# Gated linear attention with an MLP on one core: another order table for all five engines

## The chip, the cores and the metric

One Trainium2 chip, one core. The metric is the device time of one execution in microseconds (us); the time of the kernel before is the median of 3 runs.

## The reference

Inputs `q, k, v, a_re, a_im` have the shape (4, 8, 768, 48): batch, heads, sequence, head width, all fp32. Then there are `moe_g_ln` (384), `moe_w_ch1` (384, 1536) and `moe_w_ch2` (1536, 384). Cut to what is computed:

```python
mag   = sqrt(a_re**2 + a_im**2)
scale = minimum(mag, 0.999) / (mag + 1e-6)
a     = (a_re + 1j*a_im) * scale            # a complex gate for each step and channel
for t in range(768):                        # S: state, 48 x 48 for each batch and head
    S = a[t][:, None] * S + outer(k[t], v[t])
    y[t] = q[t] @ real(S)
x   = concat_heads(y)                       # (4, 768, 384)
xn  = (x - mean(x)) / sqrt(var(x) + 1e-6) * g_ln
out = x + maximum(xn @ w_ch1, 0) @ w_ch2
```

## The kernel before, in words

The sequence is cut into chunks of 128 steps, so the 4 batches of 768 steps give 24 chunks, numbered 0 to 23. Two chunks of a batch make a pair: 12 pairs, 0 to 11. Within a chunk the recurrence becomes matrix products; from chunk to chunk a state `G` is carried. The elementwise work on gates, queries and keys is done for a pair at a time (128 x 768). Pair 0 is cut in two halves by heads, so that the first work can start early.

The operations of a pair P (chunks n = 2P and 2P+1), with the names that the table uses:

- Loads: `are`, `aim` (gates, in two copies so that real and imaginary lanes stand side by side), `k`, `q`, `vf`. The weights come with `wl`.
- Magnitude of the gate, as a logarithm: `ln`, `iv` (ACT), `r`, `r2` (the ratio and its square), `u` (ACT), `l`, `lc` (DVE; `lc` is the instruction at L475, `r` and `r2` at L295 or L464).
- `dec` (PE, L483) sums the logarithms along the chunk with a triangular matrix `u_e`; `e` and `en` (ACT, L487) are the exponentials.
- Phase: `th` (arctangent, ACT), `ph` (PE sums it), `car` (the carry for the next pair), `sin`, `abs` (the tile `sh`) and `cos` (ACT; written to `trig`).
- `ke`, `qe` are keys and queries times the decay, `ks`, `qs` these times sine and cosine. DVE or POOL does them (L295). `v` casts the values.
- For each chunk: `qT`, `kT` are transposes on PE (L614) into PSUM, which `qsT`, `ksT` copy out; or `qsT` or `ksT` alone is one transposing DMA on SP's queue (L619). `am` (L637) multiplies queries and keys, `atm` masks the product, `gm` and `G` carry the state, `y` (L687, L690) forms the result, `x` copies it out, `bn` takes mean and variance, `xtr` (L708) and `xT` transpose it, on PE and by a copy, or by a DMA.
- For the pair: `rstd` (L724, L725 on ACT), the first layer `mm1` (L742) in three thirds of two parts, `relu` of each third (L759 on ACT, L761 on DVE; tile `h`), the second layer `mm2` (L774) for each chunk in three parts.
- Output of a chunk: either `ot` on DVE (L790), which scales, adds x and reads PSUM, or `oa` on ACT (L780) and then `ot` on POOL (L787). `st` (L797) stores it.

Nothing in the program chooses the order. A long string, `PLAN`, holds one token for each operation, `name:EngineBank@behind`, in the order in which all engines are to take them. The engine letter is P, A, V, G or S (PE, ACT, DVE, POOL, SP); the digit is the PSUM bank; `@x` makes a POOL operation wait until the DVE operation x is done. DMAs are issued by the engine in the token: on SP's or ACT's or POOL's queue, in that engine's order. `Graph.run` walks the string, emits each operation and asserts that what it needs stands ahead of it. A scheduling layer beneath adds the semaphores, and so every engine runs its own list in order and waits where it must. This layer is the same for both kernels, and it also puts in the waits between two engines that read one PSUM bank. The number of buffers of each tile is set by `RINGS`, which is the same in both.

PE has dummy matmuls besides, `warm.i` (L807), which fill the time before its first real work:

```python
for i in range(134):
    g.add(f"warm.{i}", lambda i=i: nc.tensor.matmul(
        bank(f"warm.{i}")[:, 0:256], lhsT=u_e[:, 0, 0], rhs=..., start=True, stop=True), ...)
```

An operation whose token is missing from the table is left out where the program has two ways to do a thing (`qT`, `kT`, `xtr`, `oa`, `tab`, `warm`): with `qsT.14:S` there is no `qT.14`, with `ot.13:V` no `oa.13`.

Of the kernel before, what the change touches and what calls it, by code (L numbers as in the profile page):

```python
# [54 lines left out]
warm.98:P2 decc.1:V4 warm.99:P2 vf.0.0:S car0.0:G warm.100:P2 warm.101:P2 warm.102:P2 mask:G warm.103:P2 warm.104:P2
aim.3.0:S tab.trig.1:A warm.105:P2 warm.106:P2 warm.107:P2 wl.0:G qe.1.0.1:V warm.108:P2 warm.109:P2 vf.0.1:S
warm.110:P2 warm.111:P2 warm.112:P2 qe.1.0.0:V warm.113:P2 warm.114:P2 pad.qs.1:G warm.115:P2 warm.116:P2 l.2.0:V
th.0.0:A warm.117:P2 warm.118:P2 wl.2:G warm.119:P2 ph.0.0:P1 th.0.1:A th.1.0:A qe.0.0.0:V ph.0.1:P4 qe.0.1.0:V
warm.120:P0 warm.121:P0 warm.122:P0 k.1.0:S car.0.0:V1 decc.0:V5 sin.0.0:A1 lc.2.0:V sin.0.1:A4 qt.0.0:P1 ks.0.0.1:V
warm.123:P0 car.0.1:A4 wgc:V cos.0.0:A1 qt.0.1:P4 ph.1.0:P6 k.1.1:S ks.0.1.1:V cos.0.1:A4 qs.0.1.1:V th.2.0:A  # L60
qs.0.0.1:V qs.0.1.0:V wp.1:P5 ks.0.1.0:V sin.1.0:A6 qs.0.0.0:V ks.0.0.0:V qT.1:P4 wc.1.2:V5 tab.log.2:A qT.0:P1
qsT.1:V4 kT.1:P0 qs.1.0.1:G@wc.1.2 dec.2.0:P2 car.1.0:V6 ln.3.0:A warm.124:P4 qsT.0:V1 warm.125:P4 wp.0:P4 e.2.0:A2
are.4.0:S wc.1.0:V5 kT.0:P1 en.2.0:A2 vf.1.0:S ksT.1:V0 ksT.0:A1 wc.0.0:V4 vf.1.1:S am.1:P2 warm.126:P0 wc.1.1:V5
iv.3.0:A warm.127:P0 am.0:P0 wc.0.2:V4 qt.1.0:P6 tab.trig.3:A warm.128:P5 warm.129:P5 warm.130:P5 warm.131:P5
wc.0.1:V4 warm.132:P5 warm.133:P5 atm.0:V0 ph.2.0:P4 r.3.0:G@wc.0.1 cos.1.0:A6 k.2.0:S v.0:A wp.2:P6 atm.1:V2
aim.4.0:S sin.2.0:A4 gm.0:P7 ke.1.0.0:G y.0:P0 G.0:V7 k.2.1:S x.0:A0 qt.2.0:P4 ke.1.0.1:V gm.1:P7 cos.2.0:A4 y.1:P1
q.2.0:S qs.1.0.0:V xtr.0:P0 ks.1.0.0:V x.1:A1 qT.2:P3 th.3.0:A ks.1.0.1:V qT.3:P5 qsT.2:V3 xtr.1:P1 q.2.1:S xT.0:A0
r2.3.0:G@ks.1.0.1 kT.3:P4 qsT.3:A5 xT.1:V1 kT.2:P2 ksT.3:V4 mm1.0.0.0:P0 G.1:V7 q.3.1:S tab.log.4:A v.1:G am.3:P4
ksT.2:V2 mm1.0.0.1:P0 are.5.0:S ke.2.0.0:G atm.3:V4 ln.4.0:A mm1.0.1.0:P2 q.3.0:S wl.3:G mm1.0.1.1:P2 relu.0.0:A0
wc.2.0:V6 am.2:P4 wc.2.2:V6 relu.0.1:A2 gm.2:P7 k.3.0:S atm.2:V4 ph.3.0:P0 qe.2.0.0:G@wc.2.2 G.2:A7 k.3.1:S iv.4.0:A  # L70
y.3:P2 wl.4:G wc.2.1:V6 y.2:P3 x.3:A2 gm.3:P7 pad.ks.2:G u.3.0:A mm1.0.2.0:P4 x.2:V3 r.4.0:G@wc.2.1 bn.3:V xtr.2:P6
xtr.3:P3 mm1.0.2.1:P4 xT.2:A6 xT.3:V3 G.3:V7 tab.trig.5:A mm1.1.1.0:P2 relu.0.2:V4 qe.2.0.1:G are.6.0:S mm1.1.1.1:P2
sin.3.0:A0 wl.5:G mm1.1.2.1:P6 bn.0:V vf.2.0:S relu.1.1:A2 mm1.1.0.1:P4 pad.qs.2:G l.3.0:V mm1.1.2.0:P6 abs.3.0:A0
r2.4.0:V mm1.1.0.0:P4 th.4.0:A car.3.0:V0 mm2.0.0:P2 relu.1.0:A4 ke.2.0.1:V mm2.1.0:P3 qs.2.0.1:V vf.2.1:S cos.3.0:A
lc.3.0:V mm2.2.0:P4 qs.2.0.0:V bn.2:V tab.log.6:A qT.4:P5 mm2.1.1:P3 bn.1:V rstd.1:G dec.3.0:P0 ks.2.0.1:V u.4.0:A
ks.2.0.0:V mm2.0.1:P2 rstd.0:G en.3.0:A0 l.4.0:V ksT.5:S mm2.2.1:P4 e.3.0:A0 lc.4.0:V ln.5.0:A relu.1.2:V6
qe.3.0.1:G@lc.4.0 mm2.1.2:P3 qe.3.0.0:G mm2.0.2:P2 aim.5.0:S oa.1:A3 qT.5:P0 iv.5.0:A vf.3.0:A ot.0:V2 dec.4.0:P6
qsT.4:V5 mm2.2.2:P4 e.4.0:A6 vf.3.1:A qs.3.0.1:V kT.4:P1 qs.3.0.0:V en.4.0:A6 dps.3:P5 are.7.0:S dps.4:P2 ksT.4:V1
ke.3.0.0:G@qs.3.0.0 qT.6:P3 qsT.5:A0 ph.4.0:P6 ot.2:V4 aim.6.0:S ke.3.0.1:G ln.6.0:A decc.3:V5 decc.4:V2 am.4:P4
q.4.0:S v.2:G qsT.6:V3 mm2.3.0:P1 iv.6.0:A atm.4:V4 ks.3.0.1:G k.4.0:S qT.7:P2 tab.trig.7:A mm2.3.1:P1 qsT.7:V2  # L80
gm.4:P3 am.5:P4 sin.4.0:A6 ks.3.0.0:V k.4.1:S y.4:P2 atm.5:V4 r.5.0:G@ks.3.0.0 kT.6:P0 car.4.0:A6 mm2.3.2:P1 x.4:A2
G.4:A3 ksT.6:V0 k.5.1:S kT.7:P5 abs.4.0:A6 xtr.4:P4 ot.1:G y.5:P0 ksT.7:V5 q.4.1:S th.5.0:A am.6:P6 x.5:V0 v.3:G
k.5.0:S am.7:P2 xT.4:A4 atm.6:V6 xtr.5:P0 ph.5.0:P4 r2.5.0:G xT.5:A0 cos.4.0:A ot.3:V1 gm.6:P0 mm1.2.1.1:P6 atm.7:V2
G.6:A0 vf.4.1:A r.6.0:G aim.7.0:S abs.5.0:A4 y.6:P1 mm1.2.1.0:P6 x.6:V1 sin.5.0:A4 vf.4.0:A mm1.2.2.1:P2 relu.2.1:V6
cos.5.0:A xtr.6:P1 r2.6.0:G y.7:P4 mm1.2.2.0:P2 th.6.0:A st.0:A x.7:V4 gm.7:P0 bn.7:V xtr.7:P4 tab.log.8:A ke.4.0.1:G
mm1.2.0.0:P6 xT.6:V1 mm1.2.0.1:P6 q.5.1:S xT.7:V4 qe.4.0.0:G G.7:V0 u.5.0:A are.8.0:S mm1.3.0.1:P4 bn.6:V ke.4.0.0:G
# [127 lines left out]
def kernel(  # L214
# [13 lines left out]
    B, H, S, D = q.shape  # L228
# [615 lines left out]
```

## Time and profile before

| | |
|---|---|
| median of 3 runs | 190.38 us (190.01, 190.38, 192.57) |
| the profiled execution | 190.44 us, its span 188.7 us |
| granted TensorE clock | 0.996 |
| busy: PE, ACT, DVE, POOL | 177.6, 159.0, 156.6, 105.0 us |
| instructions: PE, ACT, DVE, POOL | 2045, 224, 287, 124 |
| read from and written to memory | 28.31 MB, 4.72 MB |
| first layer-1 matmul (L742) starts | 36.84 us |

The span is the time from the first to the last instruction that the profiler sees; what the execution takes beyond it (1.74 us) lies around it. PE's busy time includes the dummies of the head. Busy shares are means over stages with different limits, so the stretches are to be read, not the total.

A row of the timeline gives the start, the duration, the engine, the line, the operation with its tiles and, in brackets, how long the engine was idle before it and which instruction it waited for by the profile. Where that instruction has nothing to do with it, the wait was another one.

### The profile page before, as it was taken

How to read it: one execution, taken by the hardware profiler on the slowest of the kernel's cores; microseconds unless marked ns; L12 is line 12 of the kernel's file. 1: busy time of each engine (PE TensorE's matmuls, PEld its weight loads, DVE VectorE, ACT ScalarE, POOL GpSimd, SP SyncE). 2: the span in 40 equal slices, each digit the busy share in tenths (PEclk: the TensorE clock that was granted, in tenths of full speed). 3: DMA queues.
4: the chain of work that ended last, by engine and by line, in shares of the span. 5: the costliest groups of instructions: out<-in, count | busy, mean ns of one | idle time of the engine just before them, and what ended most of it. 6: DMA issues, size and time to landing. Idle time of an engine off the chain costs nothing.

```text
span 188.7 us, 5157 instructions
## 1 busy us (share of the span) xinstructions
PE 177.6 (94%) x2045; PEld 136.7 (72%) x2045; DVE 156.6 (83%) x287; ACT 159.0 (84%) x224; POOL 105.0 (56%) x124
## 2 busy tenths in 40 slices
PE   5999789999999999999959999999999999998991
PEld 3897565888657888766747687878867777786781
DVE  2677999999999999999996988998989867775532
ACT  3969899999999999899959999998999979762340
POOL 7409233579187899080549392348784963940130
PEclk9999999999999999999999999999999999999998
DMA  6999999999969998889999999999799979994032
GB/s 162 287 258 179 220 213 203 222 221 193 238 119 300 184 227 232 156 194 237 161 269 210 191 239 235 281 225 201 137 170 250 216 124 178 248 218 148 5 125 83
DMA packets 133080, 37.57 MB, mean 199 GB/s; under 512 B 127168, under 2 KB 133056, under 8 KB 133056
## 3 DMA queue, kind: packets, MB, share of 16 engines
q1 hardware_dynamic: 107760, 27.21, 72.8%
q10 hardware_dynamic: 22512, 7.67, 17.4%
q0 software_dynamic: 2784, 2.36, 8.2%
q8 instruction: 16, 0.26, 0.6%
q14 instruction: 8, 0.07, 0.1%
HBM read 28.31 MB, written 4.72 MB: 175 GB/s over the span
## 4 chain that ended last, share of the span: by engine, by line
PE 57%; DVE 17%; DMA 7%; SPq 6%; ACT 3%; issue 3%; POOL 3%; ACTq 1%; DVEq 0%; POOLq 0%
PE banks L774 21%; PE banks L742 15%; PE banks L637 4%; DMA w2b<-in_moe_w_ch_dram 4%; SPq L451 4%; PE banks L508 3%; PE banks L614 3%; DVE w1b L394 3%; DMA q<-in_q_dram 3%; PE banks L483 2%; DVE atm L295 2%; SPq L410 2%; PE banks L687 2%; PE banks L690 2%; PE banks L665 2%
## 5 line engine op out<-in xcount | busy, mean ns | idle before, releaser
L774 PE MATMUL banks<-w2b,h 128*128 128x384 bf16 (+1 forms) x300 | 55.5, 319 | 0.7 <-ACT h L759 0.5
L742 PE MATMUL banks<-xT,w1b 128*128 128x256 bf16 x432 | 50.7, 272 | 0.2 <-ACT sh L551 0.2
L742 PEld LDWEIGHTS <-w1b 128*128 128x128 bf16 x432 | 41.4, 98 | 6.3 <-DVE xT L292 0.4
L774 PEld LDWEIGHTS <-h 128*128 128x128 bf16 x300 | 26.7, 97 | 13.6 <-ACT h L759 1.0
L295 DVE TENSOR_TENSOR atm<-banks,mask 128x1024 bf16<-128x1024 f32 x24 | 28.9, 1220 | 3.0 <-PE banks L637 2.2
L759 ACT ACTIVATE h<-banks 128x1024 bf16<-128x1024 f32 (+1 forms) x26 | 25.6, 1008 | 3.9 <-DVE ks L295 2.3
L812 ACT ACT_TABLE_LOAD x19 | 24.4, 1283 | 1.8 <-PEq L828 1.3
L295 POOL TENSOR_TENSOR ke<-k,en 128x384 bf16<-128x384 f32 x17 | 15.4, 916 | 14.9 <-ACT en L487 4.7
L807 PE MATMUL banks<-u_e 128*128 128x256 f16 x134 | 18.2, 293 | 2.2 <-POOL u_e L324 2.2
L787 POOL TENSOR_TENSOR ot<-ot,x 128x384 f32<-128x384 f32 x13 | 12.1, 936 | 14.6 <-ACT ot L780 12.4
L295 POOL TENSOR_TENSOR r<-aim,are 128x768 f16<-128x768 f32 (+1 forms) x8 | 13.7, 1715 | 10.8 <-DVE w1b L394 4.1
L295 POOL TENSOR_TENSOR qs<-qe,trig 128x768 bf16<-128x768 bf16 x8 | 13.0, 1640 | 8.4 <-DVE w1b L394 5.4
L807 PEld LDWEIGHTS <-u_e 128*128 128x128 f16 x134 | 13.9, 105 | 4.8 <-POOL u_e L324 1.9
L637 PE MATMUL banks<-qsT,ksT 128*128 128x128 bf16 x192 | 14.5, 219 | 2.5 <-DVE stats L700 1.9
L637 PEld LDWEIGHTS <-ksT 128*128 128x128 bf16 x192 | 12.0, 97 | 4.6 <-issue 2.3
L761 DVE TENSOR_SCALAR h<-banks 128x1024 bf16<-128x1024 f32 (+1 forms) x11 | 12.8, 1167 | 2.8 <-PE banks L742 2.8
L295 POOL TENSOR_TENSOR qe<-q,e 128x384 bf16<-128x384 f32 x12 | 10.9, 916 | 6.8 <-DVE r L295 3.6
L472 DVE SCALAR_TENSOR_TENSOR l<-r,w 128x768 f16<-128x768 f16 (+1 forms) x13 | 12.7, 977 | 1.7 <-ACT r L468 1.7
L700 DVE BATCH_NORM_STATS2 stats<-x 128x6 f32<-128x384 bf16 x24 | 13.1, 546 | 0.1
L454 ACT ACTIVATE w<-are 128x768 f32<-128x768 f32 (+1 forms) x13 | 10.4, 801 | 2.0 <-DMA are<-in_a_re_dram 1.5
L687 PE MATMUL banks<-v,atm 128*128 128x48 bf16 x192 | 11.9, 183 | 0.0
L687 PEld LDWEIGHTS <-atm 128*128 128x128 bf16 x192 | 10.7, 96 | 1.1 <-DVE atm L295 0.4
(101 smaller groups left out, 379.3 us busy)
## 6 DMA issues: line engine op xcount, KB each, us to landing
k<-in_k_dram SPq DMA_DIRECT2D x24, 192.0 KB, 5.0
q<-in_q_dram SPq DMA_DIRECT2D x24, 192.0 KB, 4.5
are<-in_a_re_dram SPq DMA_DIRECT2D x11, 384.0 KB, 5.4
aim<-in_a_im_dram SPq DMA_DIRECT2D x11, 384.0 KB, 4.9
out_dram<-ot ACTq DMA_DIRECT2D x19, 192.0 KB, 3.4
vf<-in_v_dram ACTq DMA_DIRECT2D x18, 192.0 KB, 4.7
w1b<-in_moe_w_ch_dram POOLq DMA_DIRECT2D x3, 384.0 KB, 7.0
vf<-in_v_dram SPq DMA_DIRECT2D x6, 192.0 KB, 6.6
```

The source lines that it names most:

```text
L295: {"DVE": nc.vector, "POOL": nc.gpsimd}[eng(name)].tensor_tensor(**kw)
L472: nc.vector.scalar_tensor_tensor(out=S_("l"), in0=S_("r2"), scalar=0.5, in1=S_("w"), op0=ALU.mult, op1=ALU.add)
L637: nc.tensor.matmul(ps[:, h], lhsT=T("ksT", n)[:, h], rhs=T("qsT", n)[:, h], start=True, stop=True)
L687: nc.tensor.matmul(ps[:, h], lhsT=T("atm", n)[:, h], rhs=T("v", P)[:, c, h], start=True, stop=nfirst)
L700: nc.vector.bn_stats(out=T("stats", n), in_=T("x", n))
L742: nc.tensor.matmul(ps[:, jj], lhsT=w1b[:, dc, ts(gi * JG + jj, C)], rhs=T("xT", P)[:, dc].rearrange("p c t -> p (c t)"), start=(dc == 0), ...
L759: act(out=dst, in_=src, func=AF.Relu)
L761: nc.vector.tensor_scalar(out=dst, in0=src, scalar1=0.0, scalar2=None, op0=ALU.max)
L774: nc.tensor.matmul(bank(own)[:, 0:w], lhsT=T("h", P)[:, j, ts(c, C)], rhs=w2b[:, j, es], start=(j == 0), stop=(j == NJ - 1))
L787: nc.gpsimd.tensor_tensor(out=T("ot", n)[:, es], in0=T("ot", n)[:, es], in1=T("x", n)[:, es], op=ALU.add)
L807: g.add(f"warm.{i}", lambda i=i: nc.tensor.matmul(bank(f"warm.{i}")[:, 0:256], lhsT=u_e[:, 0, 0], rhs=u_e[:, 1].rearrange("p j t -> p (j t ...
L812: g.add(f"tab.{nm}.{i}", lambda tab=tab: nc.scalar.preload_act_table_set(tab))
```

## The change

`PLAN` is replaced by another table with 1139 tokens in place of 1161, and the number of dummies goes from 134 to 118. Nothing else differs. Line numbers below the table are two lower in the changed kernel (L759 becomes L757).

```diff
 PLAN = """
-aim.0.0:A tab.log.0:A aim.0.1:A ue:G are.0.0:S are.0.1:S pad.e.1:G uth:V pickf:V one:G warm.0:P0 pad.ks.0:G warm.1:P0
...
+tab.log.18:A rstd.9:A ot.19:V7 oa.18:A5 mm1.10.2.0:P0 relu.10.2:A0 relu.10.0:V2 mm1.10.1.1:P6 mm1.10.1.0:P6 am.22:P4
...
 """
...
-    for i in range(134):
+    for i in range(118):
         g.add(f"warm.{i}", lambda i=i: nc.tensor.matmul(
```

What differs between the tables, by operation:

- Gone: 16 dummies, `qT.14` and `xtr.18` (`qsT.14` and `xT.18` are DMAs now), and `oa` of chunks 13, 16, 19 and 20 (their `ot` is on DVE now).
- Loads of `vf`: 18 on ACT's queue become 3, 6 on SP's become 21. Stores: 19 on ACT's queue become 11, 6 on SP's become 14.
- `ks`: 5 on POOL become 12, 21 on DVE become 14. `qe`: 12 on POOL become 16. `v`: 5 on POOL become 9.
- `ot`: 13 on POOL become 9, 12 on DVE become 16. `x`: 12 on ACT become 17. `xT`: 8 on ACT become 10. Pairs whose `rstd` is on ACT: 5 become 9.
- POOL operations that wait behind a DVE operation (`@`): 27 become 36.

The first place is the head of DVE's list. Before:

```order
L329 TENSOR_SCALAR u_th<-u_e 128x512
L339 MEMSET pick_f 128x64
L340 MEMSET pick_f 1x128
L295 TENSOR_TENSOR r_84<-aim_67,are_64 128x384
L472 SCALAR_TENSOR_TENSOR l_89<-r_87,w_82 128x384
L475 TENSOR_SCALAR l_89<-l_89 128x384
L295 TENSOR_TENSOR r_85<-aim_68,are_65 128x768
```

and now:

```order
L293 TENSOR_TENSOR r_84<-aim_67,are_64 128x384
L293 TENSOR_TENSOR r_87<-r_84 128x384
L470 SCALAR_TENSOR_TENSOR l_89<-r_87,w_82 128x384
L473 TENSOR_SCALAR l_89<-l_89 128x384
L293 TENSOR_TENSOR r_84<-aim_67,are_64 128x384
L293 TENSOR_TENSOR r_85<-aim_68,are_65 128x768
L293 TENSOR_TENSOR r_88<-r_85 128x768
```

The square of the first half (`r_87<-r_84`, which ACT did) and the ratio of the second half (which POOL did) are DVE's now; `u_th` and `pick_f` come later.

The second place is ACT's list around pair 4's relus (`h_160`). Before:

```order
L551 ACTIVATE sh_105<-banks 128x768
L797 DMA out_dram<-ot_166 128x384
L812 ACT_TABLE_LOAD
L454 ACTIVATE w_83<-are_64 128x768
L759 ACTIVATE h_160<-banks 128x1024
L797 DMA out_dram<-ot_165 128x384
L759 ACTIVATE h_160<-banks 128x1024
L487 ACTIVATE e_98<-banks 128x768
```

and now:

```order
L489 ACTIVATE th_93<-r_85 128x768
L795 DMA out_dram<-ot_165 128x384
L288 CAST x_141<-banks 128x384
L532 ACTIVATE trig_101<-banks 128x768
L524 ACTIVATE car_168<-banks 32x384
L778 ACTIVATE ot_164<-banks,rstd_154 128x384
L288 COPY xT_156<-banks 128x3x128 x2
L555 ACTIVATE trig_101<-sh_104 128x768
L795 DMA out_dram<-ot_163 128x384
L532 ACTIVATE trig_102<-banks 128x768
L524 ACTIVATE car_167<-banks 32x384
L549 ACTIVATE sh_105<-banks 128x768
```

followed there by a relu, a table load, `w` and the last relu. The store of chunk 3 (`ot_165`), which stood between the two relus, comes earlier, behind an arctangent; the x copy, the two xT copies and a carry are added.

The third place is late in ACT's list. Before, ahead of the last two relus of pair 10 (`h_160`):

```order
L759 ACTIVATE h_160<-banks 128x1024
L797 DMA out_dram<-ot_165 128x384
L797 DMA out_dram<-ot_162 128x384
L797 DMA out_dram<-ot_164 128x384
L724 ACTIVATE rstd_151<-mv_146 128x2
L725 ACTIVATE rstd_151<-rstd_151 128x2
L759 ACTIVATE h_160<-banks 128x1024
```

and now, at pair 9 (`h_161`):

```order
L555 ACTIVATE trig_103<-sh_105 128x768
L757 ACTIVATE h_161<-banks 128x1024
L795 DMA out_dram<-ot_163 128x384
L795 DMA out_dram<-ot_166 128x384
L757 ACTIVATE h_161<-banks 128x1024
L288 CAST G_128<-banks 128x384
```

The three stores are not together any more; two others (chunks 16 and 14) stand between two relus of pair 9.

More of the change, by code (lines that the diff above doesn't have):

```diff
@@ L55 @@
[L55 to L84, printed above, removed]
@@ L140 @@
[L140 to L143 removed]
+ue:G pad.e.1:G aim.0.0:A are.0.0:S tab.log.0:A ln.0.0:A iv.0.0:A are.1.0:S ln.1.0:A gln:S cmean:G are.0.1:S aim.1.0:S
```

173 lines of the change are left out of this document (100 added, 73 removed).

## The prediction

> **What bounds the kernel now.** I read the busy totals first, then a table of busy time by stretch, then the timeline at each place where TensorE (PE) stops.
>
> ```profile
> span 188.7 us, 5157 instructions
> PE 177.6 (94%) x2045; PEld 136.7 (72%) x2045; DVE 156.6 (83%) x287; ACT 159.0 (84%) x224; POOL 105.0 (56%) x124
> ```
>
> PE is the busiest, but 94% is an average; the stretches say more. Each row gives the length, then the busy time of each engine.
>
> ```profile
> core 0: us, PE busy (x) PEld busy (x) DVE busy (x) ACT busy (x) POOL busy (x), PEclk, DMA share, GB/s
> 0.00:37.00 37.00, 32.35 (x335) 25.14 (x336) 29.14 (x57) 31.55 (x48) 16.97 (x38) 1.00 1.03 219
> 37.00:60.00 23.00, 22.86 (x258) 17.16 (x256) 22.00 (x43) 22.18 (x29) 15.60 (x20) 1.00 1.07 208
> 60.00:95.00 35.00, 35.00 (x429) 27.39 (x427) 34.19 (x60) 33.73 (x46) 21.90 (x21) 1.00 1.03 204
> 95.00:100.00 5.00, 3.09 (x31) 2.19 (x30) 4.29 (x9) 2.66 (x4) 2.93 (x2) 1.00 1.06 272
> 100.00:165.00 65.00, 64.85 (x800) 49.72 (x799) 55.07 (x100) 60.36 (x85) 42.53 (x41) 1.00 1.12 206
> 165.00:188.70 23.70, 19.42 (x205) 15.14 (x202) 11.86 (x22) 8.53 (x16) 5.07 (x6) 0.97 0.41 117
> ```
>
> Until 37 us PE looks busy, but 134 of its matmuls there are dummies, so the head is set by DVE, ACT and the loads that lead to the first layer-1 matmul. From 37 us on PE is the bound: it idles 0.14 us, 0, 1.91, 0.15, and 4.28 in the last stretch, most of that the tail behind the last matmul. ACT comes next: from 37 to 95 us it is busy 55.91 of 58, 2.09 idle. Later it has more room (60.36 of 65). So four places can change the time: the head, the hole at 97 us, a small hole near 172 us, and the tail.
>
> The hole:
>
> ```profile
> 91.80 1.89 SPq L619 DMA_TRANSPOSE ksT<-ks  x1
> ksT<-ks SPq DMA_TRANSPOSE x1, 5.6
> 97.45 0.36 ACTq L797 DMA_DIRECT2D out_dram<-ot  x1
> 97.92 1.02 ACT L759 ACTIVATE h<-banks 128x1024 bf16<-128x1024 f32 x1 [2.34 <-DVE ks L295]
> 98.99 0.38 PE L637 MATMUL banks<-qsT,ksT 128*128 128x128 bf16 x4 [1.91 <-DVE stats L700]
> ```
>
> ACT sat idle 2.34 us before its relu (pair 4's last layer-1 third). The row names a DVE multiply, which touches nothing of that relu. What ACT issued just ahead of it is a store at 97.45, and a transposing DMA of SP, issued at 91.80 and 5.6 us under way, landed at 97.4. I read it so: the store waited on ACT's queue for that landing (the DMAs of SP and ACT take turns on a few completion semaphores, and these two had the same), and relu stood behind the store. PE then lacked the bank that relu frees: 1.91 us, and no other engine takes part. The small hole has the same form:
>
> ```profile
> 168.74 2.28 ACTq L797 DMA_DIRECT2D out_dram<-ot  x3
> 171.06 0.20 ACT L724 ACTIVATE rstd<-mv 128x2 f32<-128x2 f32 x1 [1.36 <-DVE G L292]
> 172.47 0.82 PE L774 MATMUL banks<-w2b,h 128*128 128x384 bf16 x4 [0.53 <-ACT h L759]
> ```
>
> Three stores on ACT's queue, ACT idle 1.36, its next relu late, PE idle 0.53.
>
> **The change part by part.** The sum goes against the profiled execution: 190.44 us, that is 188.7 of span and 1.74 around it. That is 0.06 above the median of the runs (190.38).
>
> (a) Work taken from PE. Chunk 14's query transposes (8 matmuls) and chunk 18's x transposes (3) become transposing DMAs.
>
> ```profile
> L614 PE MATMUL banks<-ident,qs 128*128 128x128 bf16 x104 | 7.6, 219 | 0.1
> L708 PE MATMUL banks<-ident,x 128*128 128x128 bf16 x72 | 7.1, 219 | 0.0
> ```
>
> By busy time per matmul (7.6/104 = 0.073, 7.1/72 = 0.099) they are 0.58 + 0.30 = 0.88; my estimate is 0.6, since single durations overlap and starts stood closer together. Bounds 0 and 0.9: they lie in a stretch where PE has no gap. The 16 dummies that go cost nothing; they fill a wait.
>
> (b) The head. On the way to the first decay matmul (L483) stands this:
>
> ```profile
> 7.42 1.00 POOL L295 TENSOR_TENSOR r<-aim,are 128x384 f16<-128x384 f32 x1 [2.76 <-ACT are L456]
> 7.55 2.12 DVE L475 TENSOR_SCALAR l<-l 128x384 f16<-128x384 f16 x1
> 8.36 0.52 POOL L362 MEMSET ks<- 128x512 bf16 x1
> 10.31 0.49 PE L483 MATMUL banks<-l,u_e 128*128 128x192 f16 x4
> 11.63 0.26 DVE L475 TENSOR_SCALAR l<-l 128x384 f16<-128x384 f16 x1
> 36.84 0.82 PE L742 MATMUL banks<-xT,w1b 128*128 128x256 bf16 x6
> ```
>
> The same DVE instruction takes 0.26 us later and 2.12 here, while POOL runs a multiply and a memset beside it. The change puts that POOL multiply (`r.0.1`) on DVE behind the instruction, the first square (`r2.0.0`) too, and DVE's two memsets of `pick_f` later. So 1.86 of stall can go, less about 0.6 for the square that DVE now does on the way: about 1.2 earlier here. Following the lists from there to 36.84, DVE's is another few tenths shorter and ACT's longer: I take 1.3. Best 2.1 (the stall gone, and DVE's shorter list all used); worst is no gain, if ACT, below, eats it. The Trainium skill, page "SBUF — State Buffer", section "Who interferes with whom", says that DVE and GpSimd share one port pair and the second to ask is blocked until the first has finished; the trace agrees at this place (2.12 against 0.26). The same rule speaks against the rest of the table, and I return to it among the rivals.
>
> (c) ACT up to the hole. Up to pair 4's last relu the new table gives ACT these more than it takes: x copies +2, xT +3, qsT +1, ksT +1, pairs of rstd steps +3, car +2; and G −2, abs −1, v −1.
>
> ```profile
> L290 ACT CAST x<-banks 128x384 bf16<-128x384 f32 x12 | 5.7, 477 | 1.7 <-PE banks L690 1.5
> L290 ACT COPY xT<-banks 128x384 bf16<-128x384 bf16 x8 | 3.8, 481 | 5.3 <-PE banks L708 5.2
> L290 ACT CAST G<-banks 128x384 bf16<-128x384 f32 x8 | 3.8, 479 | 0.0
> L418 ACT CAST v<-vf 128x768 bf16<-128x768 f32 x4 | 3.3, 834 | 0.0
> L290 ACT COPY qsT<-banks 128x1024 bf16<-128x1024 bf16 x2 | 2.1, 1027 | 0.0
> L551 ACT ACTIVATE sh<-banks 128x768 f16<-128x768 int16 x8 | 6.5, 815 | 0.0
> L526 ACT ACTIVATE car<-banks 32x384 f16<-32x384 int16 (+1 forms) x5 | 2.3, 451 | 0.2 <-issue 0.2
> L290 ACT COPY ksT<-banks 128x1024 bf16<-128x1024 bf16 x1 | 1.0, 1016 | 0.0
> L724 ACT ACTIVATE rstd<-mv 128x2 f32<-128x2 f32 x5 | 1.0, 199 | 1.8 <-DVE G L292 1.4 <-DVE mv L701 0.5
> ```
>
> That is 0.95 + 1.44 + 1.03 + 1.02 + 1.2 (two steps of 0.2, three times) + 0.90 − 0.96 − 0.82 − 0.83 = +3.9 us. Against it, ACT's idle up to that relu is 5.45 + 0.82 + 1.27 + 2.34 = 9.88, some 3 of it the start. ACT issues 6 DMAs up to there in place of 13, and the store that stood right before the relu now stands a few operations earlier, behind an arctangent. So 2.34 of store wait can go and 3.9 of work comes into about 4.5 of other waits. PE's 1.91 can vanish whole or stay; I take 1.6 of it as won, bounds 0 and 1.9.
>
> (d) The late stores. Three in a row go from ahead of the rstd that stood at 171.06; two (`st.16`, `st.14`) now stand right ahead of pair 9's last relu. The first is worth 0.53 of PE's idle and a little slack around it; the second can cost as much as ACT waited behind three, 1.36. Bounds −0.7 and +1.2; I take −0.6, since PE shows 0.15 idle in the 65 us around that relu and ACT there has 4.6 to spare.
>
> (e) The end:
>
> ```profile
> 184.39 1.27 DVE L790 SCALAR_TENSOR_TENSOR ot<-banks,rstd,x 128x384 f32<-128x384 f32 x3 [2.17 <-PE banks L774]
> ```
>
> Three output instructions, one full and two half wide, wait for PE's last layer-2 groups and take 1.27 together, then their stores go. In the new table the full row and one half stand ahead of PE's last three groups, and only one half is left behind them. Of the two thirds that then go earlier, about 0.8 us, half lies beside PE's last matmuls already (184.39 is before PE's end). I take −0.3, bounds 0 and −0.4.
>
> Costed at nothing: DVE loses net seven `ks` multiplies, POOL gets them.
>
> ```profile
> L295 DVE TENSOR_TENSOR ks<-ke,trig 128x768 bf16<-128x768 bf16 (+1 forms) x21 | 10.3, 512 | 0.8 <-POOL ke L295 0.6
> L295 POOL TENSOR_TENSOR ks<-ke,trig 128x768 bf16<-128x768 bf16 x5 | 8.2, 1641 | 5.1 <-DVE qs L295 4.9
> ```
>
> POOL pays 11.5 us for what DVE did in 3.6, but POOL is busy 105.0 of 188.7, and that idle is the cover; without it the 7.9 would come on the way to the key transposes. SP's queue takes 15 more value loads, 8 more stores and two more transposes; a store that waits there holds back the loads behind it. No row prices it; I take 0, with 0 and 1 as bounds, one store wait of 2.34 here having cost PE 1.91.
>
> Sum: −0.6 − 1.3 − 1.6 − 0.6 − 0.3 = −4.4, so 190.44 − 4.4 = **186.0 us**.
>
> **The rivals.** First, ACT becomes the bound (chance 0.28). Place: pair 4's last relu. If its waits for PE and DVE stay as long as they are and a store before it waits as now, the +3.9 comes on top of 97.92, PE waits for all of it, and the two stores before pair 9's last relu add 1.2: 190.44 − 0.9 (a and e) + 3.9 + 1.2 = 194.6 us. For it: 2.09 idle in 58 us cannot take 3.9. Against: the idle of 5.45 before 37 us can take some, and seven ACT DMAs go. It decides from the point where ACT's idle up to that relu fails to shrink by 3.9.
>
> Second, the change doesn't do what it says, and stalls only move (chance 0.18). The waits between two engines on one PSUM bank are put in by the layer under the table in both kernels; a table that knows of them wins only where they bound PE. The one such wait that I find in the waits of ACT is this:
>
> ```profile
> ACT trig L534 <- DVE car L529: 0.6, 1, 0.6
> ```
>
> 0.6 us, in the head. Then (a) and (e) stay, and half of the head: 190.44 − 0.9 − 0.6 = 188.9 us. Against it: the 1.91 and the 1.86 are seen and their causes are moved.
>
> Into this case goes the port. Stalls of 1.86 like the one at 7.55 can come where POOL's new multiplies meet DVE. DVE gets some 3.6 us of room from `ks` alone, so two such stalls are covered and each further one costs up to 1.86: four of them (0.05 within the 0.18) make 186.0 + 2 x 1.86 = 189.7. The rule of the page named above is what would make them.
>
> **How the numbers follow.** Forecast 0.54, second rival 0.18, first rival 0.28. About 2% of 190.38 (3.8 us) is what a measurement of this kernel can tell from no change: below 186.6 is faster, above 194.2 slower. The forecast sits just inside faster, with its unknowns on both sides; the sum of the best ends is −0.9 − 2.1 − 1.9 − 0.7 − 0.4 = −6.0, so 184.4, and if PE's modelled busy time hides a little waiting behind late copies, 183.0. The forecast's own range is 183.0 to 188.0. The range reaches to 194.5, about the middle of the first rival; left out are half of that (0.14) and a few hundredths below. The part of the forecast that ends above 186.6 is set off against part of the lower ends of the rivals: 0.54 faster, 0.18 within, 0.28 slower.
>
> **What would show it.** Right: the first decay matmul near 9.1 us and the first layer-1 matmul near 35.5; no PE idle over 1 us between 95 and 100; ACT's share up, and its idle ahead of pair 4's last relu under 1 us; no gap before pair 9's last relu. Wrong: PE idle spread over 37 to 95 us with ACT as releaser (first rival); DVE instructions of 2 us beside POOL multiplies (the port); a hole of 2 us behind an ACT store elsewhere (the stall moved). The forecast fails above all if step (c) does: ACT is the engine with the least room for what it is given.

## The result, and the profile after

The changed kernel takes 191.78 us (median of 20 runs, 190.37 to 195.98), the kernel before 190.47 (20 runs, 189.68 to 192.57). The ratio is 1.0062, 95% interval 1.0034 to 1.0091: slower by 0.6%, about 1.2 us, where 186.0 and "faster" were forecast. The ratios here leave out the executions that ran in the slow state, the medians do not. The profiled execution took 191.65 us.

One correction to the description of the kernel above: `are` and `aim` are loaded once each, not in two copies.

The page of the changed kernel, and busy time by the same stretches:

```profile
span 189.7 us, 5105 instructions
PE 176.9 (93%) x2018; PEld 135.7 (72%) x2018; DVE 151.4 (80%) x273; ACT 160.2 (84%) x233; POOL 108.5 (57%) x123
```

```profile
0.00:37.00 37.00, 31.16 (x316) 23.60 (x317) 28.47 (x56) 31.73 (x49) 21.59 (x45) 1.00 1.05 218
37.00:60.00 23.00, 22.96 (x264) 17.65 (x262) 21.09 (x39) 22.60 (x33) 14.24 (x13) 1.00 1.14 223
60.00:95.00 35.00, 34.30 (x412) 25.93 (x410) 33.39 (x55) 34.05 (x50) 21.92 (x20) 1.00 0.99 221
95.00:100.00 5.00, 4.93 (x55) 3.91 (x53) 3.54 (x8) 4.94 (x8) 5.00 (x5) 1.00 1.14 170
100.00:165.00 65.00, 61.84 (x747) 47.54 (x746) 50.96 (x92) 56.28 (x79) 42.10 (x39) 1.00 1.06 211
165.00:189.70 24.70, 21.68 (x243) 17.07 (x239) 13.95 (x28) 10.61 (x18) 3.66 (x5) 1.00 0.37 98
```

The hole at 97 us is gone: PE idles 0.07 of 5 us there, 1.91 before. From 60 to 95 it idles 0.70 (0 before), and from 100 to 165 us 3.16 (0.15 before). That is new, and two rows hold most of it:

```profile
147.83 0.64 SPq L408 DMA_DIRECT2D vf<-in_v_dram  x1
149.93 2.65 SPq L712 DMA_TRANSPOSE xT<-x  x1
152.90 0.56 DVE L418 TENSOR_SCALAR v<-vf 128x768 bf16<-128x768 f32 x1 [1.70 <-DMA vf<-in_v_dram]
154.45 0.34 PE L706 MATMUL banks<-ident,x 128*128 128x128 bf16 x3 [1.31 <-DVE x L290]
158.99 1.37 SPq L617 DMA_TRANSPOSE qsT<-qs  x1
164.04 0.61 PE L635 MATMUL banks<-qsT,ksT 128*128 128x128 bf16 x8 [1.54 <-DMA qsT<-qs]
```

A value load that SP issued at 147.83 held DVE 1.70 us at its cast; the copy of x stood behind the cast, and PE waited 1.31 for it. Then PE waited 1.54 for a query transpose that SP issued at 158.99. Both DMAs are on SP's queue.

To compare places in two lists I subtract from the start of a pair's first layer-1 matmul the PE work that stands ahead of it (each group of matmuls at its usual spacing in the trace of before, dummies at nothing). What is left is how late PE is, in us. The sums are mine and stand in no view:

| pair | 0 | 1 | 4 | 5 | 8 | 9 | 10 | 11 |
|---|---|---|---|---|---|---|---|---|
| before | 21.4 | 21.5 | 22.5 | 25.0 | 25.2 | 25.6 | 25.8 | 26.7 |
| changed | 21.4 | 22.1 | 24.3 | 25.0 | 25.4 | 27.3 | 29.0 | 29.0 |
| e1_values_on_act | 21.0 | 21.8 | 23.9 | 24.6 | 25.0 | 25.4 | 25.4 | 25.4 |
| e2_store_behind_relu | 21.4 | 21.5 | 23.2 | 23.8 | 25.8 | 26.3 | 26.6 | 27.3 |
| e5_before_half_values | 21.6 | 21.7 | 22.4 | 23.1 | 23.3 | 23.7 | 24.1 | 24.9 |
| e10_head_end_again | 20.9 | 22.9 | 25.1 | 25.8 | 28.3 | 29.9 | 31.9 | 31.9 |
| e16_turn_for_pool | 20.9 | 21.6 | 23.2 | 23.9 | 26.4 | 27.1 | 27.1 | 27.2 |

The changed kernel has gained nothing at pair 0, loses 1.8 by pair 4, is level when the kernel before falls into its hole, and loses 3.0 against it between pairs 8 and 10 (0.2 behind at pair 8, 3.2 at pair 10). Then it wins back 0.9. Each row is one execution; single executions of one kernel differ by up to 2 us and more, so the verdicts on time come from the ratios. The row of e1 is the fastest of its twelve executions (187.96, their median is 190.07), that of e2 is 1.2 above its median.

### The profile page after: what moved, and what is told of

Read it like the earlier page. It is cut to its first block, busy times and chain, and to the rows that moved or that the text cites. A ratio compares the mean times of both kernels' runs of the same rounds, so it can differ in the third digit from the quotient of the medians.

```text
span 189.7 us, 5105 instructions
## 1 busy us (share of the span) xinstructions
PE 176.9 (93%) x2018; PEld 135.7 (72%) x2018; DVE 151.4 (80%) x273; ACT 160.2 (84%) x233; POOL 108.5 (57%) x123
## 3 DMA queue, kind: packets, MB, share of 16 engines
q10 hardware_dynamic: 5232, 2.85, 5.3%
## 4 chain that ended last, share of the span: by engine, by line
PE 39%; DMA 15%; ACT 15%; DVE 14%; SPq 9%; issue 4%; POOL 2%; DVEq 0%; ACTq 0%
PE banks L740 13%; PE banks L772 12%; DVE atm L293 4%; DMA are<-in_a_re_dram 4%; DMA w1b<-in_moe_w_ch_dram 4%; SPq L408 3%; PE banks L506 3%; SPq L449 3%; ACT L810 3%; SPq L617 3%; DMA vf<-in_v_dram 3%; DMA qsT<-qs 3%; ACT h L757 2%; PE banks L635 2%; DMA k<-in_k_dram 2%
## 5 line engine op out<-in xcount | busy, mean ns | idle before, releaser
L772 PE MATMUL banks<-w2b,h 128*128 128x384 bf16 (+1 forms) x300 | 54.0, 320 | 0.0
L757 ACT ACTIVATE h<-banks 128x1024 bf16<-128x1024 f32 (+1 forms) x26 | 25.8, 1004 | 4.7 <-PE banks L740 4.5
L293 POOL TENSOR_TENSOR qe<-q,e 128x384 bf16<-128x384 f32 x16 | 15.2, 957 | 11.5 <-ACT e L485 7.0
L293 POOL TENSOR_TENSOR ks<-ke,trig 128x768 bf16<-128x768 bf16 (+1 forms) x12 | 17.7, 1488 | 3.8 <-ACT trig L555 2.2
L759 DVE TENSOR_SCALAR h<-banks 128x1024 bf16<-128x1024 f32 (+1 forms) x11 | 12.9, 1173 | 7.9 <-PE banks L740 7.9
L805 PE MATMUL banks<-u_e 128*128 128x256 f16 x118 | 16.8, 299 | 2.2 <-POOL u_e L322 2.2
L785 POOL TENSOR_TENSOR ot<-ot,x 128x384 f32<-128x384 f32 x9 | 8.2, 911 | 15.3 <-ACT ot L778 9.6
L805 PEld LDWEIGHTS <-u_e 128*128 128x128 f16 x118 | 12.4, 107 | 4.7 <-POOL u_e L322 1.9
L293 POOL TENSOR_TENSOR r<-aim,are 128x768 f16<-128x768 f32 x7 | 12.6, 1811 | 4.8 <-DVE l L473 3.0
L288 ACT CAST x<-banks 128x384 bf16<-128x384 f32 x17 | 8.1, 480 | 7.6 <-PE banks L688 6.8
L293 POOL TENSOR_TENSOR qs<-qe,trig 128x768 bf16<-128x768 bf16 (+1 forms) x7 | 10.7, 1534 | 3.7 <-ACT trig L532 3.5
L452 ACT ACTIVATE w<-are 128x768 f32<-128x768 f32 (+1 forms) x13 | 10.3, 798 | 2.5 <-DMA are<-in_a_re_dram 2.5
```

The source lines that it names most:

```text
L293: {"DVE": nc.vector, "POOL": nc.gpsimd}[eng(name)].tensor_tensor(**kw)
L452: add(f"ln.{X}", lambda S_=S_: act(out=S_("w"), in_=S_("are"), func=AF.Ln), needs=[f"are.{X}"], uses=[("are", P), ("w", P)])
L757: act(out=dst, in_=src, func=AF.Relu)
L759: nc.vector.tensor_scalar(out=dst, in0=src, scalar1=0.0, scalar2=None, op0=ALU.max)
L772: nc.tensor.matmul(bank(own)[:, 0:w], lhsT=T("h", P)[:, j, ts(c, C)], rhs=w2b[:, j, es], start=(j == 0), stop=(j == NJ - 1))
L785: nc.gpsimd.tensor_tensor(out=T("ot", n)[:, es], in0=T("ot", n)[:, es], in1=T("x", n)[:, es], op=ALU.add)
```

## The experiments

All ratios are to the kernel before, run on the same chip beside them.

### The late holes: SP's queue

**e1_values_on_act**, on the changed kernel:

```diff
-vf.9.0:S  vf.9.1:S  vf.10.0:S  vf.10.1:S  vf.11.1:S  vf.11.0:S
+vf.9.0:A  vf.9.1:A  vf.10.0:A  vf.10.1:A  vf.11.1:A  vf.11.0:A
```

> The changed kernel with the six value loads of pairs 9 to 11 back on ACT's queue (SP issues them in the changed kernel), nothing else. In the changed kernel PE has two late holes: about 1.5 us behind the x transposes at 154.45 (DVE's value cast waited 1.70 for a value load that landed at 152.8) and about 1.7 at 164.04 (waits for a query transpose that SP issued at 158.99). Theory 1, SP's queue is full: between 130 and 160 us it issues without a pause, so loads and transposes behind it come late. Then both holes go or shrink together: PE idle from 150 to 166 us from 3.0 to under 1.2 us, the time from 191.8 to 189 to 190. Theory 2, only the value load is late and the query transposes take their 5 us anyway: the first hole goes, the second stays at 1.5, time about 190.4. Rival 3, the loads block ACT's queue instead: a new hole behind ACT, time 191.5 or more.

190.07 us, ratio 0.9944 (0.9905 to 0.9982): 1.7 less than the changed kernel, and faster than the kernel before. Busy time from 150 to 166 us, of the changed kernel and of this one:

```profile
150.00:166.00 16.00, 13.15 (x152) 9.50 (x151) 8.67 (x13) 9.61 (x14) 9.27 (x8) 1.00 0.91 195
150.00:166.00 16.00, 15.93 (x197) 11.93 (x195) 12.43 (x22) 11.18 (x17) 10.24 (x9) 1.00 0.95 201
```

PE idles 0.07 in place of 2.85: both holes are gone. Theory 1 holds: the query transpose has no data from those loads, and without them it is issued 2.9 us earlier (158.99 in the changed kernel):

```profile
149.33 1.19 SPq L712 DMA_TRANSPOSE xT<-x  x1
156.10 1.32 SPq L617 DMA_TRANSPOSE qsT<-qs  x1
```

Of the 2.9 us, 0.6 are the earlier start of the x transpose, 1.5 the shorter time that this transpose holds the queue (1.19 against 2.65), and 0.7 the load that no longer stands behind it. Once issued, the query transpose is also 1.7 us less under way (3.2 against 4.9). Why one and the same DMA holds the queue longer, or lands later, no run shows.

**e14_before_values_on_sp**: the same six tokens, in the kernel before, from A to S.

> The kernel before with one part of the change alone: the six value loads of pairs 9 to 11 on SP's queue in place of ACT's. Theory SP: SP has room there (in the kernel before it issues fewer DMAs: 103 rows of its list against 133), so it costs only 0 to 1.0 us from 190.3; late holes before a transposing DMA of at most 1. If it costs 1.0 to 3.0 the loads on SP are harmful by themselves, whatever else stands there. Rival: it is faster, since ACT has six DMAs less to wait for (189.3 or less).

191.05 us, 1.0037 (1.0003 to 1.0072), at the lower end of what was expected. PE now has two waits that the kernel before lacks:

```profile
160.91 0.61 PE L637 MATMUL banks<-qsT,ksT 128*128 128x128 bf16 x8 [0.62 <-DMA qsT<-qs]
162.88 0.61 PE L637 MATMUL banks<-qsT,ksT 128*128 128x128 bf16 x8 [0.71 <-DMA qsT<-qs]
```

So this part of the change alone makes holes at the query transposes, of half the size, where SP has fewer other DMAs (110 on its queue against 136). But the way there is another: SP issues these two at 155.50 and 156.90, as in the kernel before (155.53 and 156.88), and they land 0.6 and 1.5 later. The loads on SP cost time in two ways, by their place in the queue (e1) and by later landing (here). The profiled execution is 0.9 above the median.

**e9_x_transpose_on_pe**, on the changed kernel: `xT.18:S` becomes `xtr.18:P6 xT.18:V6`.

> The changed kernel with chunk 18's x transpose back on PE (three matmuls) and its copy on DVE; in the changed kernel it is a transposing DMA on SP's queue. There SP holds at that DMA until x of chunk 18 is there (149.9), takes 2.65 us for it, and then issues eight DMAs without a pause until the query transpose at 158.99 for which PE stands still (1.70). Theory SP: that queue is the last link, so the query transpose is issued 1.2 to 2.7 us earlier and the hole at 162 us shrinks from 1.7 to under 0.7; PE pays 0.3 for the transpose; the time falls from 191.8 to 190.2 to 191.2. Rival: the hole depends on when the query itself is ready, or on DMA landing: hole and time stay (191.6 to 192.2).

191.81 us, 1.0036 (0.9956 to 1.0116): unclear, with four executions from 189.43 to 192.65, and the profile is of the slowest. So the part of the x transpose is open.

**e15_stores_on_act**, on the changed kernel: `st` of chunks 8 to 12 and 15 from S to A.

> The changed kernel with six stores (chunks 8 to 12 and 15) on ACT's queue in place of SP's; the value loads stay on SP. Theory SP, issue time as such: six DMAs of about 0.6 us less on SP bring the late transposes forward by 2 to 3 us, as the six loads did in e1_values_on_act, and the time is 189.5 to 190.7. Rival: stores wait for their data and for a completion semaphore and hold ACT behind them; then ACT shows idle of 1 to 2 us behind a store and the time is 191.5 or more.

191.51 us, 1.0048 (1.0004 to 1.0092): hardly better than the changed kernel. The wait of 1.54 for the query transpose at 164 is gone, but three others of 0.8 to 1.0 stand elsewhere (PE for a query transpose at 136.5, for x at 155.8, for the mask at 165.5). The time is what the rival said, but ACT's idle of 1 to 2 us behind a store is not there. SP's issue time as such is not the whole story.

**e13_all_values_on_act**, on the changed kernel: all 16 value loads of pairs 4 to 11 on A.

> The changed kernel with all 16 value loads of pairs 4 to 11 on ACT's queue in place of SP's (e1_values_on_act had the last six: 190.1, from 191.8). Theory SP: every DMA taken off SP brings its transposing DMAs forward; no wait of PE for a query or key transpose over 0.3 us is left and the time is 187.5 to 189.5. Rival 1, only the last third of SP's queue matters: 189.5 to 190.5, as e1_values_on_act. Rival 2, ACT is held by its own DMAs waiting (as by the store at 97 us in the kernel before): new idle of ACT over 1 us behind a load, 190.5 or more.

194.51 us, 1.0223 (1.0178 to 1.0268): rival 2. No wait of PE for a transposing DMA is left, but ACT is held:

```profile
126.51 0.38 ACTq L408 DMA_DIRECT2D vf<-in_v_dram  x1
130.89 0.83 ACT L416 CAST v<-vf 128x768 bf16<-128x768 f32 x1 [2.71 <-DMA vf<-in_v_dram]
132.16 0.36 PE L663 MATMUL banks<-v,ks 128*128 128x48 bf16 x8 [1.93 <-ACT G L288]
```

On ACT the load is issued only when ACT's list has come to it, and the cast that wants it starts 4.4 us after that. The packed trace, which names the semaphores, shows a second price: six of ACT's value loads go within 0.1 us of the landing of a DMA of SP that had the same completion semaphore, in the changed kernel none. How much of the 2% each of the two makes is open.

### The hole at 97 us, and whether DMA is a second bound

**e2_store_behind_relu**, on the kernel before: the token `st.3:A` moves from ahead of `relu.4.2:A2` to behind it.

> The kernel before with one token moved: the store of chunk 3 goes behind pair 4's last relu on ACT's queue, not ahead of it. Theory (the prediction's reading): the store waited at 97.45 for a completion semaphore and held relu, PE idled 1.91 for it. Then the hole between 95 and 100 us goes (PE idle there under 0.4) and the time falls from 190.5 to about 188.6, or to about 189.5 if ACT, busy without a pause up to there, makes PE wait a little later. Rival: the wait was the one that the row names (DVE), and then the hole stays at 1.9 and the time at 190.5.

190.15 us, 0.998 (0.9944 to 1.0016). The reading of the hole was right: PE is busy all of 95 to 100 us. The semaphores in the trace of before say the same: the store takes number 107, one of eight that the DMAs of SP and ACT share, and the transposing DMA had it until it landed at 97.43. But the time did not follow. In the profiled execution (191.3) another store did the same later:

```profile
124.00 1.08 SPq L410 DMA_DIRECT2D q<-in_q_dram  x1
129.67 0.36 ACTq L797 DMA_DIRECT2D out_dram<-ot  x1
130.13 0.48 ACT L290 CAST x<-banks 128x384 bf16<-128x384 f32 x1 [2.18 <-DMA q<-in_q_dram]
```

The query load, issued at 124.00, landed at 129.65; the store went out at 129.67, and ACT stood 2.18 us. Both have semaphore 104. In the kernel before the same load was issued at 121.94, landed at 126.48, and this store did not wait. Why the load came later in e2 is not shown.

**e5_before_half_values** and **e7_late_store_half_values**: the kernel before, and e2's, with this change. It leaves out the values of four of eight heads from pair 2 on, so the output is not the reference's.

```diff
-out=T(nm, P)[:, c],
+out=T(nm, P)[:, c, 0:4 if nm == "vf" and P > 1 else H],
```

> The kernel before, but the value loads of pairs 2 to 11 bring heads 0 to 3 only (heads 4 to 7 of v are left out and old data is used): 20 loads of 0.1 MB in place of 0.2, about 2 of 37.6 MB and 10240 of 133080 packets less; every instruction's order is the same. Theory D, the 16 DMA engines are a second bound (busy share 0.96 to 1.22 in every stretch from 20 to 170 us): loads and transposing DMAs land sooner, the store at 97.4 waits less, and the time falls by 1 to 2.5 us from 190.5. Rival: DMA is hidden and only the order of waits matters; then the time stays within 0.5 us of 190.5.

> The kernel before with the store of chunk 3 behind pair 4's last relu (as in e2_store_behind_relu) and with the values of heads 4 to 7 not loaded from pair 2 on. In that run the hole at 97 us went, but a new one of 2.18 us on ACT came at 130, behind a store that waited for a query load landing at 129.65 (5.7 us under way). Theory D, DMA gave the gain back: with less to move both holes are small, PE idle from 60 to 150 us under 0.8, and the time is 187.5 to 188.7, lower than with the cut alone. Rival, the second hole is of another cause: it stays, and the time is that of the cut alone.

188.80 us, 0.9937 (0.989 to 0.9984), and 188.45, 0.9941 (0.9891 to 0.9991). With 5% fewer bytes, and the order the same, the hole at 97 us is gone in the first as well (busy time from 95 to 100 us):

```profile
95.00:100.00 5.00, 5.00 (x55) 3.62 (x54) 4.83 (x9) 4.98 (x7) 2.95 (x2) 1.00 1.10 282
```

and in the second the one at 130 too. This looks like theory D, the 16 DMA engines as a second bound: their share is about 1 in every stretch up to 165 us. The trace of e5 does not bear it out at this hole. At 91 us PE and DVE are where they are in the kernel before, within 0.1 us, and then:

```profile
91.71 1.59 SPq L619 DMA_TRANSPOSE ksT<-ks  x1
92.63 0.36 ACTq L797 DMA_DIRECT2D out_dram<-ot  x1
```

The transposing DMA is 5.9 us under way and lands at 97.61, no sooner than before (97.43). The store goes 5 us ahead of that, because it has another semaphore here: 104, free since 90.54, while the transposing DMA has 110. The table is the same, so with the smaller loads the layer beneath it deals the semaphores out otherwise. The hole is all that e5 gains: PE's delay is 0.1 less than before at pair 4, 1.9 less at pair 5 and 1.8 less at pair 11. So the gain goes with the semaphore that is no longer shared, and that 5% of the bytes gave it is not shown. That the store's move adds nothing to the cut (e7, against its theory D) fits: the wait at 97 us was gone already. Whether the DMA engines bound the kernel is open.

**e6_after_half_values**: the changed kernel with this cut.

> The changed kernel with the same cut: values of heads 4 to 7 are not loaded from pair 2 on. Theory D: the two late holes (1.5 us at 153, 1.7 at 163), which end with a value load and a transposing DMA that land late, shrink to under half, and the time falls from 191.8 to 188 to 189.5, more than the kernel before gains, as SP's queue also gets shorter issues. Theory SP, what counts is only the time that SP takes to issue: a load of half the size issues faster, so it cannot be told from D by the time alone, but then the latencies from issue to landing stay (median 3.9 to 4.3 us) and only issue times move. Rival: no effect, 191.5 or more.

190.12 us, 1.0025 (0.9982 to 1.0067). The hole at the value cast went: the load of half the size lands 2.8 us after its issue, 5.0 in the changed kernel, and has the same semaphore in both. The one at the query transpose stayed, 1.47 us: SP issues eight DMAs in a row from the x transpose on, whatever their size. So the first was a matter of landing, and the second mostly one of SP's order.

### The head

**e8_before_head**: in the kernel before, `r2.0.0` and `r.0.1` go to DVE (V), `uth` and `pickf` behind them.

> The kernel before with one piece of the change: the ratio of pair 0's second half goes from POOL to DVE, the square of the first half from ACT to DVE, and u_th and pick_f behind them. Prediction's step (b): the 2.12 us instruction of DVE takes 0.3, the first decay matmul comes at 8.6 to 9.2 (10.31 before). If the lists are what sets the head, the first layer-1 matmul comes 0.5 to 1.3 us earlier than 36.84 and the time falls by 0.3 to 1.3. Rival, the loads set the head (DMA busy share 1.0 from the start; in e4_head_end DVE waited 3.07 us for a key load): the first layer-1 matmul stays within 0.3 of 36.84 and the time at 190.5.

190.54 us, 1.0008 (0.9967 to 1.0049). DVE's instruction took 0.26, as foreseen, and was done at 8.48; yet the first decay matmul came at 10.80. In PE's list 56 dummies stand ahead of it.

**e11_before_head_fewer_dummies**: 20 of these 56 left out, `uth` and `pickf` behind `lc.0.0`.

> The kernel before with the head piece of e8_before_head, u_th and pick_f now behind the first decay input, and 20 of the 56 dummy matmuls ahead of the first decay matmul left out. In e8_before_head the decay input was done at 8.48 and the first decay matmul came only at 10.80, behind the dummies. Theory: dummies in PE's list ahead of it were the bound, so the first decay matmul comes at 8.4 to 9.0; the first layer-1 matmul follows by 0.3 to 1.0 (36.84 before) if the lists set the head, the time by as much. Rival, loads set it: the decay matmul is early, the first layer-1 matmul stays within 0.3 of 36.84, the time at 190.2 to 190.6.

193.83 us, 1.0218 (1.0163 to 1.0273). The decay matmul came at 8.04, 2.3 us earlier, but the first layer-1 matmul at 38.29, later by 1.45. Of the kernel before and of this one:

```profile
23.00:26.00 3.00, 3.00 (x33) 2.06 (x33) 2.97 (x9) 2.97 (x5) 0.61 (x1) 1.00 1.21 192
23.00:26.00 3.00, 3.00 (x15) 1.47 (x13) 2.04 (x8) 2.70 (x4) 0.00 (x0) 0.53 1.21 202
```

```profile
19.78 1.03 DVE L295 TENSOR_TENSOR qe<-q,e 128x384 bf16<-128x384 f32 x2 [0.88 <-DMA q<-in_q_dram]
```

Two things stand in the way. DVE waited for a query load, so the sines came no earlier (21.24; 21.12 before). And PE, now without work for most of 20 to 23 us (0.92 busy, 1.90 before), got a clock of 0.53 for the next 3 us: 15 matmuls where 33 ran before. The Trainium skill, page "TensorE: Matmul & The Clock Gate", section "What's actually happening", says that the clock falls to half after an idle window of about 3.4 us; this trace agrees on the half (0.53), while the longest idle of PE that its rows show there is 2.39 us. The dummies are not free to leave out. A clock of 0.53 for 3 us is worth about 1.4 us of PE's work (3 x 0.47, an estimate), as much as the 1.45 at the first layer-1 matmul; where the rest of the 3.7 us comes from (193.83 against 190.09 of the kernel before beside it) is open.

**e4_head_end** and **e10_head_end_again**, on the changed kernel. Both move `qsT.2` from ACT to DVE behind `xT.1` and `xtr.0`, `xT.0` forward; e4 also puts the weight load `wl.2` ahead of POOL's multiplies, e10 instead `wp.2` behind the first layer-1 matmuls.

> The changed kernel with the last steps before the first layer-1 matmul changed: the load of the last third of w1 goes ahead of POOL's multiplies (it is issued at 28.8 us in the changed kernel, 19.2 before, and PE waits for it at 36.2), the copy of chunk 2's query transposes goes from ACT to DVE behind xT.1, and x of chunk 0 is transposed one place earlier. The first decay matmul is 1.7 us earlier in the changed kernel (8.63), yet the first layer-1 matmul is not (36.86). Theory: the gain is there on DVE (xT.1 is done at 35.28, 36.58 before) and is lost on ACT, which does a 1.05 us copy ahead of xT.0, and on POOL's late weight load. Then the first layer-1 matmul starts at 35.8 to 36.3. The time follows by 0.5 to 1.0 if PE keeps it, or not at all if ACT bounds the stretch behind it. Rival: something else (the loads' landing) sets it and it stays at 36.8.

> The changed kernel, the end of the head once more, without moving the weight load (which in e4_head_end made the key loads late): chunk 2's query copy goes from ACT to DVE behind xT.1, x of chunk 0 is transposed one place earlier and copied first, and the matmuls that fold the last third of w1 stand behind the first layer-1 matmuls in place of ahead. Theory: DVE's xT.1 (35.28) and ACT's xT.0 then allow the first layer-1 matmul at 35.8 to 36.4 (36.86 in the changed kernel), and the time falls by 0.3 to 1.0 from 191.8. Rival: PE loses it again before 95 us, since DVE has 0.7 us more there and DMA lands no sooner: first layer-1 matmul early, time 191.5 to 192.5.

194.93 us (1.0228, 1.0181 to 1.0276) and 195.39 (1.0301, 1.0244 to 1.0359). In e4 the key loads came later: DVE waited 3.07 us for one, and the first layer-1 matmul went to 38.60. In e10 it came at 35.69, the 1.2 us that step (b) had promised, and was lost at once, and more after it; what makes the late waits longer than in the changed kernel is not shown:

```profile
37.45 0.62 PE L635 MATMUL banks<-qsT,ksT 128*128 128x128 bf16 x8 [0.94 <-DVE ksT L290]
127.23 0.62 PE L635 MATMUL banks<-qsT,ksT 128*128 128x128 bf16 x8 [1.02 <-DMA ksT<-ks]
166.95 0.61 PE L635 MATMUL banks<-qsT,ksT 128*128 128x128 bf16 x8 [1.82 <-DMA qsT<-qs]
```

### From 40 to 95 us

**e3_act_relieved**, on the changed kernel: `x.7`, `xT.7`, `x.9`, `xT.9` from A to V.

> The changed kernel with four copies taken from ACT back to DVE, as before the change: x and xT of chunks 7 and 9, about 1.9 us of ACT. Theory A, in the changed kernel ACT bounds the stretch up to pair 4's last relu (busy 93.3 of the first 100 us, 90.1 before; PE falls behind by 1.8 us more from 40 to 95 us, in steps under 0.8): pair 4's first layer-1 matmul comes 0.7 to 1.7 us earlier than 92.6 and the time is 0.5 to 1.5 less than 191.8. Theory B, the losses there are chances of order (DVE late with x, banks), not ACT's sum: no earlier than 92.3, time 191.5 or more, and DVE's added 1.8 us can make it later.

193.52 us, 1.0153 (1.0106 to 1.02): theory B. Pair 4's first layer-1 matmul came 1.1 us later, not earlier; PE waited for DVE's x (0.58 at 71.5) and xT (0.80 at 73.9). ACT's sum does not bound this stretch alone; DVE is about as full (33.39 of 35 us from 60 to 95 us, ACT 34.05).

**e16_turn_for_pool**: e1's table with `qe.6.0.1:G` become `qe.6.0.1:G@lc.7.0`. In the changed kernel these rows lie beside each other:

```profile
87.20 1.79 POOL L293 TENSOR_TENSOR qe<-q,e 128x384 bf16<-128x384 f32 x2
88.10 1.70 DVE L470 SCALAR_TENSOR_TENSOR l<-r,w 128x768 f16<-128x768 f16 x1
90.72 0.34 PE L706 MATMUL banks<-ident,x 128*128 128x128 bf16 x3 [0.58 <-DVE x L290]
```

> e1_values_on_act (190.1; the changed kernel with the value loads of pairs 9 to 11 on ACT's queue) with one wait added: POOL's second query multiply of pair 6 waits until DVE's decay input of pair 7 is done. In all profiles of this family DVE's multiply at 88 us takes 1.6 to 1.7 us beside these POOL multiplies (0.98 on average), and PE then idles 0.5 to 0.6 for DVE's copy of x at 90.7. Theory, the shared port: DVE's multiply takes 0.95, PE idle at 90 us is under 0.1, pair 4's first layer-1 matmul comes 0.5 to 0.7 earlier than in e1_values_on_act (92.14), and the time is 189.2 to 189.9. Rival, ACT or DVE are full there as such: the instruction is short, but pair 4's first layer-1 matmul stays at 92.0 to 92.4 and the time at 190.

189.87 us, 0.9954 (0.9926 to 0.9983). The DVE instruction took 1.05 and pair 4's first layer-1 matmul came at 91.46, 0.68 earlier than in e1:

```profile
87.64 1.05 DVE L470 SCALAR_TENSOR_TENSOR l<-r,w 128x768 f16<-128x768 f16 x1
```

So about 0.7 of the 1.8 us were this meeting of POOL and DVE, the prediction's port. The time stayed at e1's: in this execution PE waited 1.4 us in all for key transposes between 120 and 155, where e1's, its fastest, did not wait.

**e12_all_mended**: e1's loads, `xtr.18` on PE, e10's head, and the three dummies in pair 1's work left out.

> The changed kernel with what the runs point to: value loads of pairs 9 to 11 on ACT's queue (e1_values_on_act, 190.1), x of chunk 18 transposed on PE, the three dummies among pair 1's work left out (0.5 us of PE at 42.4), and the end of the head as in e10_head_end_again. Theory SP: no late hole in any run, 187.5 to 189.3, faster than the kernel before (190.4). Rival, DMA paces it: holes come back elsewhere, 189.5 to 190.5.

190.19 us, 0.9987 (0.9929 to 1.0046): no late hole, but the rest of PE's delay was there by pair 4 (24.8). It is no better than e1 (theory SP had 187.5 to 189.3). The faster versions are e1 and e16, by 0.5% under the kernel before and 1% under the changed one.

## Why the prediction was wrong

**(a), −0.6, right on PE and wrong in what it left out.** The eleven matmuls went; the two DMAs that took their place are in the queue that became the bound. The prediction named that queue and costed it at 0, bounds 0 and 1. This is the term that failed: 3.0 us of new delay between pairs 8 and 10 in the profiled execution, 1.7 us of the medians, as e1 shows by taking six loads off it. It also named the wrong thing, a store that waits: here loads and transposes hold the queue by being issued, and land later. The reason given, that SP has no row with a price, was the sign to look at what SP issues and when; the rows of L619 showed waits of up to 6.5 us there. That the dummies that go "cost nothing" was a second term without a price. It held here (clock 1.00 in the head); e11 shows that it need not.

**(b), −1.3, measured 0.** The stall went (0.66 in place of 2.12) and the first decay matmul came at 8.63 (forecast 9.1), a gain of 1.7. It lived until the phase sums (21.26 against 22.65) and on DVE to `xT.1` (done at 35.28; 36.58 before). It was lost on what stands beside that chain:

```profile
28.78 0.80 POOL L368 DMA_DIRECT2D w1b<-in_moe_w_ch_dram  x1
35.00 1.05 ACT L288 COPY qsT<-banks 128x1024 bf16<-128x1024 bf16 x1
35.89 0.54 ACT L288 COPY xT<-banks 128x384 bf16<-128x384 bf16 x1
36.22 0.81 PE L388 MATMUL banks<-w1b,gc 128*128 128x512 bf16 x3 [0.34 <-DMA w1b<-in_moe_w_ch_dram]
36.86 0.82 PE L740 MATMUL banks<-xT,w1b 128*128 128x256 bf16 x6
```

ACT's new copy stands ahead of `xT.0`, and POOL, busy with three new `ks`, issues the last third of w1 9.6 us later than before (19.21). Also the stall was not what held the first decay matmul before: it was done at 9.67, the dummies at 10.3. That the matmul came near the forecast is luck: the new table has 31 dummies ahead of it in place of 56, and e8, which takes the stall away and leaves the dummies, has it at 10.80. And the worst case "if ACT eats it" is what happened in part: the 3.9 us of new ACT work of step (c) begin ahead of the first layer-1 matmul.

**(c), −1.6, measured about 0.** The mechanism was right (e2, and the shared semaphore in the trace), the hole went, and its time was lost before it, in steps. Of the 1.8 us up to pair 4 the port explains about 0.7 (e16); this is the effect that the prediction put into its second rival with 0.05. The rest is open: e3 shows only that moving work from ACT to DVE makes it worse. The first rival, ACT alone, is not borne out.

**(d), −0.6, came in the profiled execution.** PE idles nowhere from 165 us to its last matmul at 186.67, where the kernel before lost 0.53 at 172.47, and between pairs 10 and 11 the changed kernel wins back 0.9. The two stores ahead of pair 9's last relu cost nothing (ACT idled 0.28 there). The form of the small hole was not the same as that at 97 us: the trace of before shows no shared semaphore there, the three stores held ACT by the 2.28 us of their own issue.

**(e), −0.3, measured −0.7.** From PE's last matmul (186.67) to the end it is 3.0 us, 3.75 before; this is past the bound of −0.4, and why is not shown.

Taken together in the two profiled executions, with (a) as estimated: 0 at pair 0, 0.2 up to pair 8, 3.0 to pair 10, −0.9 to pair 11, −0.6 for (a), −0.7 for (e), +1.0 in all, which is the difference of the spans (189.7 and 188.7).

**The rivals.** "Stalls only move" is the one that came nearest in what happened, though its 188.9 is 2.9 too low, since it left out what the queue adds. What was missing among the rivals is SP's queue as a bound of its own. The prediction quoted a DMA share of about 1 in every stretch and used none of these numbers; whether they matter is still open.

## What to carry to other kernels

When DMAs change queue, follow what stands behind each on the new queue, and what the old queue had guaranteed about the time of issue. Look up which completion semaphore a DMA shares, and with what: a test that changes the size of a load can deal the semaphores out anew, and then its gain need not be that of the bytes (e5). And a gain at the start of a chain counts only if every input of its last step, loads and other engines' copies too, comes earlier.

## What the runs showed that was not expected

With 20 dummies left out PE got a clock of 0.53 for 3 us, and the time went to 1.0218 of the kernel before (1.0008 in e8, with all dummies). With half of the value loads left out, 5% of the bytes, the time fell by 0.6% (0.2 to 1.1%), though the DMA that had been waited for landed no sooner. A store on ACT's queue held ACT's arithmetic 2.2 to 2.3 us until an unrelated DMA of SP's with the same completion semaphore had landed, twice: at 97.4 in the kernel before and at 129.65 in e2, and each time the store went within 0.03 us of the landing.
